# Copies out of PSUM that write runs of bf16 and read PSUM with a stride; the first chunk's weights read in place

## The chip, the cores and the metric

The kernel runs on one core of a Trainium2 chip. The metric is device time in microseconds (us) of one execution. The core's engines each take their instructions in order: TensorE (PE in the profile, its weight loads PEld), VectorE (DVE), ScalarE (ACT), GpSimd (POOL) and SyncE (SP), which here only issues DMAs. [...]

## The reference

Two independent parts share one program, and their outputs stand side by side.

```python
def _A_ref(x, wqkv, wo):                       # S=2048, D=640, H=32 heads of 20
    W, dil = 8, 2                              # 8 positions back, every second one
    qkv = (x @ wqkv) ...; q, k, v = qkv[0], qkv[1], qkv[2]
    logits = einsum("bhsd,bhswd->bhsw", q, kg) * scale    # kg, vg: gathered windows
    attn = softmax(logits); o = einsum("bhsw,bhswd->bhsd", attn, vg)
    return o.reshape(B, S, D) @ wo
def _B_ref(u, A_re, ..., log_dt, Dskip):       # L=2048, D=640, N=192
    P = exp(logdA[:, :, None] * l);  K = einsum("dn,dnl,dn->dl", Cc, P, dB).real
    Yf = rfft(pad(u)) * rfft(pad(K));  y = irfft(Yf)[:L]
    return y + u * Dskip
return concatenate([a, b], axis=-1)
```

Part A is a sliding-window attention with a dilation of 2; part B is a long convolution whose filter K is made from complex powers, carried out as a Fourier transform in two matmul steps each way.

## The kernel before

Part A projects q, k and v in `PartA.proj` (300 matmuls at L463 in groups of five, each group emptied by one of 60 ACT copies at L464), writes them to DRAM, and then works through eight blocks of 256 positions: `fetch` (DMAs, among them 20 of `vb` for each block), `logits` (DVE products at L503, matmuls at L505, softmax on ACT), `av` (DVE products at L529, matmuls at L532, ACT copies `oT` at L535) and `out_proj` (matmuls at L544, ACT copies `ob` at L545).

Part B works in five chunks of 128 channels. `Tables` holds for one chunk the tables of powers X and Y, which DVE builds by complex products (`cmul`, L260 to L265; `ypos`, `yneg`, `xtab`). `kgen` turns them into the filter with 512 small matmuls for a chunk (L342, L347) and four ACT copies into `Kd` (L349). `spread` sorts `Kd` into `K` (L372, copies at L375). `f1` and `f2` are the two steps of the forward transform: `f1` has 16 matmuls and eight ACT copies into `A1` (L385, L386); `f2` has 128 matmuls (L400) and 16 ACT copies into the spectrum `Sp` (L404). `Sp` is laid out as [half, signal, t, k] with 32 values of k next to each other; each copy of `f2` brings four k for 64 t of one signal, or for 64 t of both signals. `product` multiplies the spectra on DVE (L414, L415), `swap_halves` makes `UT` by a DMA, and `ia` is the first inverse step, with 64 matmuls (L427) and eight ACT copies into `Z` (L428), which is laid out with 32 t next to each other. `inverse` is the last step, at the end of the program, fed by DMAs of `HB`, `zq` and `uq`.

One iteration for chunk c does `swap_halves`, `spread(c)`, `f1`, `f2`, `product`, `ia`, then makes the tables and the filter of chunk c+2, then attention blocks 2c and 2c+1. The order on each engine is not that of the code: the body is scheduled by a timeline of estimated costs, so instructions of independent parts are mixed, and a changed dependence can move many of them. What is fixed by buffers: `f2`, `f1`, `ia`, `kgen` and `spread` share four PSUM buffers (tag "b"), and the tables X and Y have one buffer each, so a chunk's tables can be loaded only after the `kgen` of the chunk before.

Before the loop, the weights product `Gt` is made by DVE in `weights()`, and ACT copies its first chunk into slot 6 of `Xg` (L662), from where `xtab` reads it; the other chunks go through DRAM (`Gdram`).

A row "ACT CAST Sp<-ps_f 128x512" names line, engine and shape as the profile flattens them.

Of the kernel before, what the change touches and what calls it, by code (L numbers as in the profile page):

```python
# [250 lines left out]
def cmul(nc, O, Y, g, t, conj, rep=None):  # L251

    V = nc.vector
    sh = list(Y.shape)
    gr, gi = (g[:, r] for r in range(2))
    for _ in range(2):
        gr, gi = gr.unsqueeze(1), gi.unsqueeze(1)
    full = lambda ap: ap.rearrange("p a n r m -> p a (n r) m") if rep else ap
    gb = lambda ap: ap.to_broadcast([sh[0], sh[1], sh[2] * 2 if rep else 2, sh[-1]])
    V.tensor_tensor(out=full(O), in0=full(Y), in1=gb(gr), op=A.mult)  # L260
    V.tensor_tensor(out=full(t), in0=full(Y), in1=gb(gi), op=A.mult)
    P = [O[:, :, r] if not rep else O[:, :, :, r] for r in range(2)]
    T = [t[:, :, r] if not rep else t[:, :, :, r] for r in range(2)]
    V.tensor_tensor(out=P[0], in0=P[0], in1=T[1], op=(A.add if conj else A.subtract))
    V.tensor_tensor(out=P[1], in0=P[1], in1=T[0], op=(A.subtract if conj else A.add))  # L265


class Tables:
# [37 lines left out]
            neg = Y[:, 8 - 8 * i:16 - 8 * i, 1]  # L306
            V.tensor_scalar(out=neg, in0=neg, scalar1=-1.0, scalar2=None, op0=A.mult)

    def xtab(self):
        nc, X, Xg, tmp = self.nc, self.X, self.Xg, self.tmp()  # L310
        cmul(nc, X[:, 0:1], Xg[:, 6:7], self.Y[:, 32], tmp[:, 0:1], True)

        def xs(o, i, g):
            n = len(range(20)[i])
            cmul(nc, X[:, o], X[:, i], Xg[:, g], tmp[:, 0:n], True)

        S_ = slice
        xs(S_(1, 2), S_(0, 1), 2)
        xs(S_(2, 4), S_(0, 2), 1)
        xs(S_(4, 8), S_(0, 4), 0)  # L320
        xs(S_(8, 12), S_(0, 4), 3)
        cmul(nc, X[:, 12:16].rearrange("p (a b) r m -> p a b r m", a=2), X[:, 0:16].rearrange("p (a b) r m -> p a b r m", a=2)[:, :, 0:2], Xg[:, 4],
             tmp[:, 0:4].rearrange("p (a b) r m -> p a b r m", a=2), True, rep=2)
        xs(S_(16, 18), S_(0, 9, 8), 5)
        xs(S_(18, 20), S_(12, 15, 2), 5)

    def kgen(self):

        nc, X, Y = self.nc, self.X, self.Y
        MM = nc.tensor.matmul  # L330
        Kd = self.pools["keep"].tile([128, 2, NB, 16], bf16, name="Kd", tag="Kd", bufs=2)
        for q in range(4):
            t0 = 8 * q
            ps = self.pools["psum"].tile([128, 8, NB], f32, name="ps_k", tag="b", bufs=4)
            MM(ps[:], lhsT=self.pools["zero"], rhs=Y[:, 0:8, 0, 0:NB], start=True, stop=False, skip_group_check=True)
            for part in range(4):
                for i in range(8):
                    for g in range(4):
                        o = ps[32 * g:32 * g + 20, i, :]
                        if part < 2:  # L340
                            col = 32 * g + t0 + i
                            MM(o, lhsT=X[:, :, part, col], rhs=Y[:, :, part, col], start=False, stop=False,  # L342
                               tile_position=(0, 32 * g), skip_group_check=True)
                        else:
                            col = 128 + 32 * (g % 2) + t0 + i
                            hb = 64 * (g // 2)
                            MM(o, lhsT=X[hb:hb + 64, :, part - 2, col], rhs=Y[hb:hb + 64, :, part - 2, col], start=False, stop=(part == 3),  # L347
                               tile_position=(hb, 32 * g), skip_group_check=True)
            nc.scalar.copy(out=Kd[:, q // 2, :, 8 * (q % 2):8 * (q % 2) + 8].rearrange("p b t -> p t b"), in_=ps[:])  # L349
        for g in range(4):  # L350
            r = 32 * g
            nc.gpsimd.dma_start(out=Kd[r + 20:r + 32, :, 0:NB - 1, :].rearrange("p h b t -> p h (b t)"), in_=Kd[r + 8:r + 20, :, 1:NB, :].rearrange("p h b t -> p h (b t)"))
        return Kd
# [35 lines left out]
def f2(tc, pools, C, A1, Sp, s0, s1):  # L389

    nc = tc.nc
    n = 64 * (s1 - s0)
    for q in range(8):
        ps = [pools["psum"].tile([128, 4, n], f32, name="ps_f2", tag="b", bufs=4) for _ in range(2)]
        for kk in range(4):
            k = 4 * q + kk
            for r in range(2):
                for h in range(2):
                    hs = slice(64 * h, 64 * h + 64)
                    nc.tensor.matmul(ps[h][:, kk], lhsT=C["T"][hs, k, 64 * (1 - r):64 * (1 - r) + 128], rhs=A1[hs, k, r, s0:s1, :].rearrange("p s t -> p (s t)"),  # L400
                                     start=(kk == 0 and r == 0), stop=(r == 1), tile_position=(64 * h, 0), skip_group_check=True)
        for h in range(2):
            o = Sp[:, h, s0:s1, :, 4 * q:4 * q + 4].rearrange("p s t k -> p k (s t)")
            nc.scalar.copy(out=o, in_=ps[h][:])  # L404


def swap_halves(nc, Sp, UT):
# [10 lines left out]
def ia(tc, pools, C, P, Q, Z):  # L418

    nc = tc.nc  # L420
    for h in range(2):
        for tq in range(4):
            ps = pools["psum"].tile([128, 4, 128], f32, name="ps_ia", tag="b", bufs=4)
            for i in range(4):
                for n_, X in enumerate((P, Q)):
                    t = 4 * tq + i
                    nc.tensor.matmul(ps[:, i], lhsT=X[:, h, 4 * t:4 * t + 4, :].rearrange("p g k -> p (g k)"), rhs=C["E"][:, n_, :], start=(i == 0 and n_ == 0), stop=(n_ == 1), skip_group_check=True)  # L427
            nc.scalar.copy(out=Z[:, :, 16 * h + 4 * tq:16 * h + 4 * tq + 4].rearrange("p x t -> p t x"), in_=ps[:])  # L428


class PartA:
# [119 lines left out]
def kernel(  # L551
# [17 lines left out]
    nc = tc.nc  # L569
# [70 lines left out]
    t0 = tabs[0] = Tables(tc, pools, 0)  # L640
# [18 lines left out]
    t1.ymag(ta, pin)  # L659
    magnitudes(tc, pools, ta, am, 1, 5)  # L660
    Gt = weights()
    nc.scalar.copy(out=t0.Xg[:, 6], in_=Gt[:, 0])  # L662
    t0.xtab()
    Kds[0] = t0.kgen()
    for ct in range(5):
        a.proj("k", ct)
# [23 lines left out]
    def spec():  # L690
        return fp.tile([128, 2, 2, 64, 32], bf16, name="Sp", tag="Sp", bufs=2)

    U = uload(0)
    f1(tc, pools, C, U, "BU", A1, 1)
    SU = spec()
    f2(tc, pools, C, A1, SU, 1, 2)
    a.open(att)
    a.fetch(0)
# [26 lines left out]
    for c in range(NCH):  # L725
# [9 lines left out]
        f1(tc, pools, C, K, "BK", A1, 0)  # L735
        Sp = spec()
        f2(tc, pools, C, A1, Sp, 0, 1 if last else 2)
        product(nc, Sp, SU, UT)
        if c < 3:
            Z = fp.tile([128, 128, 32], bf16, name="Z", tag="Z")  # L740
        else:
            Z = Z34[:, c - 3]
        ia(tc, pools, C, Sp[:, :, 0], UT[:], Z)
        if c < 3:
            nc.sync.dma_start(out=Zd[c][:], in_=Z[:])
# [56 lines left out]
```

## Time and profile before

| | |
|---|---|
| time of the runs | median 681.76 us of 2 (679.98 to 683.54) |
| the profiled execution | 680.84 us, of which the span of its instructions is 679.0 us |
| mean granted clock of PE | 0.672 of full speed |
| DMA | 74.41 MB, mean 110 GB/s |
| POOL busy | 36.3 us (5%) |

A page of the profile gives each engine's busy time, the groups of equal instructions with their count, busy time in all, mean time of one and the idle time before them with what ended it, and the chain of work that ended last. "Busy" of a group counts overlapping instructions once, so the mean of one is longer than busy time divided by count where an engine starts the next before the last has ended. The program has three stretches: from 0 to about 182 us the loads, the tables of chunk 0 and 1 and the projections; to about 616 us the loop; the rest is the last step of the inverse.

### The profile page before, as it was taken

The numbers are of one execution on the slowest core, as the hardware profiler recorded it, in microseconds if no ns is written. First come the engines' busy times: TensorE is split into PE (matmuls) and PEld (weight loads), VectorE is DVE, ScalarE is ACT, GpSimd is POOL, SyncE is SP. The second block draws the span as 40 slices with busy tenths as digits, with TensorE's granted clock in tenths as the row PEclk, the third lists the DMA queues.
The fourth block names the chain that finished last, engine by engine and source line by source line (L and its number), as shares of the span: only waits on it lengthen the run. The fifth ranks groups of instructions, "written<-read, shape, count | busy, mean of one in ns | idle before, by whom it ended". The sixth has DMA issues, their size and how long they took to land.

```text
span 679.0 us, 12860 instructions
## 1 busy us (share of the span) xinstructions
PE 387.0 (57%) x5356; PEld 235.1 (35%) x5364; DVE 310.2 (46%) x479; ACT 491.4 (72%) x601; POOL 36.3 (5%) x80
## 2 busy tenths in 40 slices
PE   2764986885675536474525855437876247464422
PEld 1231453334443314343303633325533224242311
DVE  0965967691376525228635066471361412500000
ACT  3679776542699997659989569969699799793211
POOL 6500003000100000010000100000100000000000
PEclk9995988895558557567556685556676568567567
DMA  9811457547666631636201672113691050007995
GB/s 239 162 45 71 155 178 225 169 159 126 120 99 152 73 74 40 188 66 72 57 11 28 172 126 47 32 47 85 198 230 42 0 116 30 1 1 168 262 206 112
DMA packets 184761, 74.41 MB, mean 110 GB/s; under 512 B 135072, under 2 KB 176656, under 8 KB 183168
## 3 DMA queue, kind: packets, MB, share of 16 engines
q1 hardware_dynamic: 181296, 68.17, 43.6%
q0 software_dynamic: 2352, 5.18, 2.8%
q8 instruction: 42, 0.69, 0.4%
q10 hardware_dynamic: 1056, 0.25, 0.2%
q14 instruction: 15, 0.12, 0.1%
HBM read 44.20 MB, written 21.01 MB: 96 GB/s over the span
## 4 chain that ended last, share of the span: by engine, by line
ACT 46%; PE 17%; SPq 11%; DMA 10%; DVE 10%; issue 5%; DVEq 0%; POOL 0%; ACTq 0%; POOLq 0%
ACT Sp L404 25%; ACT Z L428 11%; PE ps_p L463 3%; SPq L723 3%; PE ps_op L544 3%; SPq L445 3%; SPq L685 3%; DMA Gdram<-cs 2%; PE ps_k L347 2%; ACT mag L299 2%; PE ps_k L342 2%; ACT A L386 2%; DMA uq<-in_B_u_dram 1%; DVE p L529 1%; DMA Ytab<-Gdram 1%
## 5 line engine op out<-in xcount | busy, mean ns | idle before, releaser
L404 ACT CAST Sp<-ps_f 128x512 bf16<-128x512 f32 (+1 forms) x96 | 183.8, 2331 | 4.1 <-PE ps_f L400 4.1
L400 PE MATMUL ps_f<-A,cT 64*128 64x128 bf16 (+1 forms) x768 | 62.4, 263 | 73.5 <-ACT Sp L404 70.1
L428 ACT CAST Z<-ps_ia 128x512 bf16<-128x512 f32 x40 | 92.0, 2743 | 8.9 <-PE ps_ia L427 8.8
L463 PE MATMUL ps_p<-xT,w 128*128 128x512 bf16 x292 | 79.3, 418 | 21.0 <-ACT st L464 15.1
L529 DVE TENSOR_TENSOR p<-vb,attn 128x2048 bf16<-128x2048 bf16 x40 | 47.8, 1221 | 70.9 <-PE ps_o L532 48.6
L503 DVE TENSOR_TENSOR prod<-qb,kb 128x2048 bf16<-128x2048 bf16 x40 | 47.9, 1225 | 70.1 <-PE ps_l L505 64.3
L400 PEld LDWEIGHTS <-cT 64*128 64x128 bf16 x768 | 46.1, 120 | 97.2 <-issue 97.1
L349 ACT CAST Kd<-ps_k 128x264 bf16<-128x264 f32 x20 | 25.8, 1325 | 40.7 <-PE ps_k L347 40.7
L464 ACT CAST st<-ps_p 128x512 bf16<-128x512 f32 x60 | 34.1, 582 | 27.2 <-PE ps_p L463 27.1
L463 PEld LDWEIGHTS <-w 128*128 128x128 bf16 x300 | 30.5, 105 | 64.7 <-issue 36.1
L544 PE MATMUL ps_op<-wo,oT 128*128 128x320 bf16 x160 | 43.1, 423 | 16.2 <-ACT oT L535 15.8
L427 PE MATMUL ps_ia<-cE,Sp 128*128 128x128 bf16 x160 | 30.1, 274 | 32.5 <-ACT Z L428 21.3
L721 ACT CAST ysb<-ps_ib 128x384 bf16<-128x384 f32 (+1 forms) x24 | 11.9, 523 | 46.9 <-PE ps_ib L720 33.0
L386 ACT CAST A<-ps_f 128x512 bf16<-128x512 f32 x80 | 42.0, 648 | 3.9 <-PE ps_f L385 3.8
L713 DVE TENSOR_TENSOR uq<-uq,Dsb 128x1536 bf16<-128x1536 bf16 (+1 forms) x8 | 6.6, 825 | 74.8 <-DMA uq<-in_B_u_dram 73.5
L347 PE MATMUL ps_k<-Ytab,Xtab 64*20 64x33 bf16 x1280 | 27.9, 244 | 14.9 <-issue 14.8
L414 DVE TENSOR_TENSOR UT<-Sp,UT 128x2048 bf16<-128x2048 bf16 x10 | 12.1, 1223 | 48.1 <-ACT Sp L404 48.1
L342 PE MATMUL ps_k<-Ytab,Xtab 128*20 128x33 bf16 x1280 | 27.0, 250 | 10.4 <-issue 5.8
L532 PE MATMUL ps_o<-p,cHs 128*32 128x256 bf16 x320 | 25.9, 377 | 9.6 <-DVE p L529 9.6
L427 PE MATMUL ps_ia<-cE,UT 128*128 128x128 bf16 x160 | 30.3, 275 | 0.0
L544 PEld LDWEIGHTS <-oT 128*128 128x128 bf16 x160 | 17.9, 127 | 33.3 <-ACT oT L535 18.2
L347 PEld LDWEIGHTS <-Xtab 64*20 64x20 bf16 x1280 | 22.5, 123 | 19.0 <-issue 16.8
(106 smaller groups left out, 645.6 us busy)
## 6 DMA issues: line engine op xcount, KB each, us to landing
vb<-vd SPq DMA_DIRECT2D x160, 64.5 KB, 2.2
HB<-k_HB SPq DMA_DIRECT2D x8, 1024.0 KB, 6.2
UT<-Sp SPq DMA_DIRECT2D x10, 512.0 KB, 5.6
Gdram<-cs SPq DMA_DIRECT2D x11, 288.0 KB, 2.9
Zdram<-Z SPq DMA_DIRECT2D x3, 1024.0 KB, 5.2
zq<-Zdram SPq DMA_DIRECT2D x12, 256.0 KB, 7.0
kb<-kd SPq DMA_DIRECT2D x8, 337.5 KB, 5.4
Xg<-Gdram SPq DMA_DIRECT2D x4, 672.0 KB, 6.5
```

The costliest lines, as they stand in the source:

```text
L342: MM(o, lhsT=X[:, :, part, col], rhs=Y[:, :, part, col], start=False, stop=False, tile_position=(0, 32 * g), skip_group_check=True)
L347: MM(o, lhsT=X[hb:hb + 64, :, part - 2, col], rhs=Y[hb:hb + 64, :, part - 2, col], start=False, stop=(part == 3), tile_position=(hb, 32 * ...
L386: nc.scalar.copy(out=A1[:].rearrange("p k r s t -> p (k r) s t")[:, :, sig, 8 * q:8 * q + 8], in_=ps[:])
L400: nc.tensor.matmul(ps[h][:, kk], lhsT=C["T"][hs, k, 64 * (1 - r):64 * (1 - r) + 128], rhs=A1[hs, k, r, s0:s1, :].rearrange("p s t -> p (s ...
L404: nc.scalar.copy(out=o, in_=ps[h][:])
L427: nc.tensor.matmul(ps[:, i], lhsT=X[:, h, 4 * t:4 * t + 4, :].rearrange("p g k -> p (g k)"), rhs=C["E"][:, n_, :], start=(i == 0 and n_ == ...
L428: nc.scalar.copy(out=Z[:, :, 16 * h + 4 * tq:16 * h + 4 * tq + 4].rearrange("p x t -> p t x"), in_=ps[:])
L463: nc.tensor.matmul(ps[:], lhsT=self.w[which][:, kt, 128 * ct:128 * ct + 128], rhs=self.xT[:, kt, 512 * sc:512 * sc + 512], start=(kt == 0) ...
L464: nc.scalar.copy(out=st[:, sc], in_=ps[:])
L503: V.tensor_tensor(out=pr[:], in0=q[:, ct].unsqueeze(1).to_broadcast([128, W, PB]), in1=windows(k[:, ct, 0:PB], 2, W), op=A.mult)
L529: V.tensor_tensor(out=p2[:], in0=windows(v[t][:, :, 0:PB], 2, 2), in1=at[:].unsqueeze(2).to_broadcast([128, 2, 4, PB]), op=A.mult)
L544: nc.tensor.matmul(ps[:], lhsT=oT[:, t, 128 * s:128 * s + 128], rhs=self.wo_sb[:, t, 320 * eh:320 * eh + 320], start=(t == 0), stop=(t == 4))
```

## The change

In three copies out of PSUM the two sides are exchanged: before, PSUM was read in the order in which it lies and SBUF was written with a stride; now SBUF is written in runs and PSUM is read with a stride. The destination and the values are the same, and so is the number of elements. `Kd` (L349) is now written in runs of 8 bf16, `Sp` (L404) and `Z` (L428) in runs of 4. The strides of the reads are 33 f32 in `kgen`, 64 or 128 f32 in `f2`, and 128 f32 in `ia`.

The fourth edit takes away the copy of `Gt` into `Xg`: `xtab` gets `Gt[:, 0:1]` as an argument and reads it where DVE made it.

```diff
-    def xtab(self):
+    def xtab(self, w=None):
         nc, X, Xg, tmp = self.nc, self.X, self.Xg, self.tmp()
-        cmul(nc, X[:, 0:1], Xg[:, 6:7], self.Y[:, 32], tmp[:, 0:1], True)
+        cmul(nc, X[:, 0:1], Xg[:, 6:7] if w is None else w, self.Y[:, 32], tmp[:, 0:1], True)
...
-            nc.scalar.copy(out=Kd[:, q // 2, :, 8 * (q % 2):8 * (q % 2) + 8].rearrange("p b t -> p t b"), in_=ps[:])
+            nc.scalar.copy(out=Kd[:, q // 2, :, 8 * (q % 2):8 * (q % 2) + 8], in_=ps[:].rearrange("p t b -> p b t"))
...
-            o = Sp[:, h, s0:s1, :, 4 * q:4 * q + 4].rearrange("p s t k -> p k (s t)")
-            nc.scalar.copy(out=o, in_=ps[h][:])
+            o = Sp[:, h, s0:s1, :, 4 * q:4 * q + 4].rearrange("p s t k -> p (s t) k")
+            nc.scalar.copy(out=o, in_=ps[h][:].rearrange("p k x -> p x k"))
...
-            nc.scalar.copy(out=Z[:, :, 16 * h + 4 * tq:16 * h + 4 * tq + 4].rearrange("p x t -> p t x"), in_=ps[:])
+            nc.scalar.copy(out=Z[:, :, 16 * h + 4 * tq:16 * h + 4 * tq + 4], in_=ps[:].rearrange("p t x -> p x t"))
...
-    nc.scalar.copy(out=t0.Xg[:, 6], in_=Gt[:, 0])
-    t0.xtab()
+    t0.xtab(Gt[:, 0:1])
```

The scheduled order moves with it. On DVE, after the last product of `weights()`, stood three groups of the gates `cs` of the next batch, and then the first product of `xtab`, which read `Xg`:

```order
L242 TENSOR_SCALAR ph<-wi 128x192
L247 TENSOR_TENSOR cs<-cs,am 128x384
L245 SCALAR_TENSOR_TENSOR ab<-ph 128x192
L242 TENSOR_SCALAR ph<-wi 128x192
L247 TENSOR_TENSOR cs<-cs,am 128x384
L245 SCALAR_TENSOR_TENSOR ab<-ph 128x192
L260 TENSOR_TENSOR Xtab<-Xg,Ytab 128x384
L261 TENSOR_TENSOR krtmp<-Xg,Ytab 128x384
```

Now the products of `xtab` follow at once, reading `Gt`:

```order
L260 TENSOR_TENSOR Xtab<-Gt,Ytab 128x384
L261 TENSOR_TENSOR krtmp<-Gt,Ytab 128x384
L264 TENSOR_TENSOR Xtab<-Xtab,krtmp 128x192
L265 TENSOR_TENSOR Xtab<-Xtab,krtmp 128x192
L260 TENSOR_TENSOR Xtab<-Xtab,Xg 128x384
```

So `xtab` of chunk 0 moves ahead of six gate instructions, and on PE the `kgen` of chunk 0 stands 50 projection matmuls earlier.

On ACT, at the end of the loop, the last `ia` (Z) and the first copies of `inverse` (`ysb`) had copies of the last attention block (`oT`, `ob`) between them:

```order
L404 CAST Sp<-ps_f_7320 128x4x64
L535 CAST oT<-ps_o 128x512 x2
L428 CAST Z_6126<-ps_ia 128x4x128 x4
L535 CAST oT<-ps_o 128x256
L428 CAST Z_6126<-ps_ia 128x4x128 x4
L545 CAST ob<-ps_op 128x320 x2
L721 CAST ysb<-ps_ib 128x384 x3
L545 CAST ob<-ps_op 128x320 x2
L721 CAST ysb<-ps_ib 128x384 x13
```

Now the attention copies all stand before the last `f2`:

```order
L404 CAST Sp<-ps_f_7319 128x64x4
L428 CAST Z_6125<-ps_ia 128x128x4 x8
L720 CAST ysb<-ps_ib 128x384 x16
L720 CAST ysb<-ps_ib 128x512 x8
```

What moved are five copies of the last attention block, with the matmuls that feed them. In between, the copies of attention and of the transforms are mixed in another order too, with the same members. The line numbers after L662 are lower by one in the changed kernel.

## The prediction

> **What bounds the kernel now.** I read the page's busy times first, then its chain of work that ended last, then the same chain and the busy times for the loop alone.
>
> ```profile
> span 679.0 us, 12860 instructions
> PE 387.0 (57%) x5356; PEld 235.1 (35%) x5364; DVE 310.2 (46%) x479; ACT 491.4 (72%) x601; POOL 36.3 (5%) x80
> ...
> ACT 46%; PE 17%; SPq 11%; DMA 10%; DVE 10%; issue 5%; DVEq 0%; POOL 0%; ACTq 0%; POOLq 0%
> ```
>
> ACT is the busiest engine and holds 46% of the chain. The busy times by stretch (columns: stretch, its length, PE, PEld, DVE, ACT and POOL with counts, granted clock, DMA share, GB/s) show where:
>
> ```profile
> 0.00:182.00 182.00, 120.48 (x1526) 61.67 (x1536) 113.62 (x230) 108.28 (x221) 28.90 (x64) 0.83 0.57 151
> 182.00:616.00 434.00, 248.41 (x3593) 159.41 (x3588) 191.87 (x243) 372.21 (x358) 7.38 (x16) 0.60 0.37 80
> 616.00:679.00 63.00, 18.13 (x247) 13.97 (x245) 4.68 (x6) 10.92 (x22) 0.00 (x0) 0.69 0.86 196
> 218.00:255.00 37.00, 15.35 (x141) 9.39 (x141) 17.05 (x24) 37.00 (x20) 0.00 (x0) 0.50 0.50 74
> ```
>
> In the loop (182 to 616) ACT is busy for 372 of 434 us; in one `f2` (218 to 255) it is busy without a gap, while PE idles at a clock of 0.50. The start and the end are bound by other things: in the last 63 us the DMA engines are at 0.86 and ACT at 11 us. The chain of the loop alone, and its longest pieces (start, length, what):
>
> ```profile
> by line: ACT Sp L404 38.8%; ACT Z L428 17.8%; issue 6.3%; PE ps_op L544 4.0%; PE ps_k L347 3.8%; PE ps_k L342 3.4%; ACT A L386 2.6%; DVE p L529 1.9%; ACT mag L299 1.8%; DMA Ytab<-Gdram 1.4%; DMA out_dram<-ob 1.3%; PE ps_ia L427 1.3%; DVE kr
> ...
> 422.61 22.43 ACT Sp L404 x10
> 541.76 18.10 ACT Z L428 x8
> ```
>
> So 38.8% and 17.8% of 434 us, 168.4 + 77.3 = 245.7 us, are two of the changed copies, back to back, with nothing else ending last. The other 188.3 us of the loop are everything else.
>
> **The price of a copy.** The groups of ACT's copies out of PSUM, with mean times:
>
> ```profile
> L404 ACT CAST Sp<-ps_f 128x512 bf16<-128x512 f32 x64 | 146.3, 2724 | 1.8 <-PE ps_f L400 1.8
> L428 ACT CAST Z<-ps_ia 128x512 bf16<-128x512 f32 x40 | 92.0, 2743 | 8.9 <-PE ps_ia L427 8.8
> L386 ACT CAST A<-ps_f 128x512 bf16<-128x512 f32 x80 | 42.0, 648 | 3.9 <-PE ps_f L385 3.8
> L404 ACT CAST Sp<-ps_f 128x256 bf16<-128x256 f32 x32 | 37.5, 1546 | 2.4 <-PE ps_f L400 2.4
> L464 ACT CAST st<-ps_p 128x512 bf16<-128x512 f32 x60 | 34.1, 582 | 27.2 <-PE ps_p L463 27.1
> L349 ACT CAST Kd<-ps_k 128x264 bf16<-128x264 f32 x20 | 25.8, 1325 | 40.7 <-PE ps_k L347 40.7
> ```
>
> All read PSUM in order. L464 writes without a gap, L386 in runs of 8 bf16, and both are near 0.6 us for 512 elements. L404, L428 and L349 write every element apart from the next, and cost over four times as much. What is slow is the lone write. Back to back, a copy of 512 takes 146.3/64 = 2.29 us and one of 256 takes 37.5/32 = 1.17 us, so a lone element costs (2.29 − 1.17)/256 = 4.4 ns, and a copy in runs of 8 goes at 42.0/80 = 0.525 us, 1.03 ns per element.
>
> Runs of 4 appear nowhere. From below: they can't beat runs of 8, 0.525 us. From above: a run could cost what its elements did singly, 2.29 us. I take one lone-write price per run, 128 × 4.4 ns = 0.56 us: that is close to the row of L386, where 64 such prices would be 0.28 us and the stream of elements sets the time. For 256 elements it is about 0.30 us, for `Kd` (runs of 8) 0.525 × 264/512 = 0.27 us.
>
> The read is the unknown. No row here reads PSUM with a stride. From below it costs nothing (L464's rate), from above I know only the lone write of 4.4 ns; it could be more, since nothing excludes it. I take nothing, because the nearest rows, L464 and L386, read the same f32 from PSUM at about 1 ns per element, and what made L404 slow was on the side of the write.
>
> [...]
>
> **The sum.** When ACT no longer ends last in these stages, PE does. Its pace is in these rows: with free buffers, and waiting for ACT in pieces of eight (L427 likewise from the chain):
>
> ```profile
> 409.71 1.89 PE L400 MATMUL ps_f<-A,cT 64*128 64x128 bf16 x32
> ...
> 415.51 1.01 PE L400 MATMUL ps_f<-A,cT 64*128 64x128 bf16 x8 [1.24 <-ACT Sp L404]
> ...
> 181.49 1.03 PE L400 MATMUL ps_f<-A,cT 64*128 64x64 bf16 x32
> 453.09 1.05 PE ps_ia L427 x8
> ```
>
> 1. `f2` on both signals, four times: 16 copies × 0.56 = 9.0 us on ACT; 128 matmuls on PE at 1.89/32 = 0.059 us take 7.6 us, at up to 0.107 us 13.7. I take 14, with the hand-overs between the four PSUM buffers: 56 us.
> 2. `f2` on one signal, twice: 16 × 0.30 = 4.8 us against 128 × 1.03/32 = 4.1 us. I take 7: 14 us.
> 3. `ia`, five times: 8 × 0.56 = 4.5 us against 64 matmuls, eight in about 0.8 before their tail, so 6.4 us. I take 7: 35 us.
>
> These 105 us stand where 245.7 stood: 140.7 us go.
>
> 4. Given back: work that lay under the copies. The waits of the loop and one chunk's stretch:
>
> ```profile
> DVE prod L503 <- PE ps_l L505: 64.3, 12, 13.9
> DVE UT L414 <- ACT Sp L404: 48.1, 7, 14.7
> ...
> 313.00:410.00 97.00, 49.99 (x860) 32.07 (x861) 49.40 (x70) 79.02 (x82) 2.61 (x6) 0.60 0.41 76
> 389.10 6.19 DMA Ytab<-Gdram
> ```
>
> A period of 97 us holds 49.4 us of DVE and 50.0 of PE. Taking out (37 − 14) + (18 − 7) leaves about 63 us. Both still fit, but DVE is then 78% busy, and its chain has a fixed part: tables come by DMA only after the `kgen` before (6.19 us), DVE builds them between attention products, and only then the next `kgen` runs. What is late next is DVE's products and PE behind them. I give back 5 us for each of four periods, 20 us; ends 0 (all fits) and 50 us (no overlap regained: half of the 88 us of DVE that lie inside the four `f2` windows).
>
> 5. `Kd`: 20 copies lose about 1 us each, but 16 of them wait for PE (the group's idle time, 40.7 us, is longer than its 25.8 us of work); on the chain 1 us appears in the first stretch. I take 0.
> 6. The copy of `Gt` and `xtab`:
>
> ```profile
> 54.23 1.16 DVE L211 TENSOR_TENSOR Gt<-pr,pr 128x960 bf16<-128x960 f32 x1
> 62.72 0.26 DVE L242 TENSOR_SCALAR ph<-wi 128x192 int32<-128x192 int32 x1 [7.33 <-ACT cs L244]
> ...
> 63.54 0.49 ACT L662 COPY Xg<-Gt 128x384 bf16<-128x384 bf16 x1
> ...
> 90.79 1.28 PE L342 MATMUL ps_k<-Ytab,Xtab 128*20 128x33 bf16 x64
> ```
>
> `Gt` is ready at 55.4, the copy runs at 63.5, and DVE idles for 7.33 us between. `xtab` will start some 9 us earlier in that gap, and the first `kgen` (90.79) can follow 50 matmuls earlier. But the stretch ends with all projections done on PE, whose total doesn't change, and with the loads behind them. I take 0, ends −5 and +3.
> 7. The tail: the five attention copies that leave the last `ia` were free there; the loads that bound the last 63 us stay. 0.
>
> The profiled execution took 680.84 us, of which 1.84 lie outside the span; it is 0.9 below the median of two runs. 680.84 − 140.7 + 20 = 560.1. I forecast 560 us.
>
> **The rivals.**
>
> [...]
>
> *Nothing gained.* If a strided read costs as much as a lone write, 4.4 ns, the copy stays at 2.29 us and the time at 681 us. For it: one such penalty is in these rows already, on the other memory. Against it: that is the extreme of what a row shows.
>
> *Slower.* If a strided read costs more than the lone write, ACT still ends last, and the 245.7 us grow in proportion. At 5 ns per element they grow by 14%, to 280 us: 715 us. It decides from 4.65 ns on, where the growth of 5.6% on 245.7 us is 2% of the whole.
>
> *All of it.* If copies go at 0.525 us, PE at 0.059 us and nothing is given back, `f2` takes 9.5 and 5, `ia` 5: 73 us, a gain of 173, 508 us. Against it: PE and DVE both need more than half of the shrunken period.
>
> **How the numbers follow.** The forecast's case (copies near 0.56 us, 530 to 585 us) has a chance of 0.62; the first rival (585 to 630) 0.18; all of it (below 530) 0.06; nothing gained 0.07; slower 0.07. A range from 520 to 615 leaves out the last two, the upper edge of the first rival and the lower of the fourth, about 0.2. About 2% is what a measurement of this kernel can tell from no change: faster 0.62 + 0.18 + 0.06 = 0.86, within 2% 0.07, slower 0.07.
>
> **What would show it.** Right: the groups of L404 and L428 have means below 0.85 us and busy times near 0.6 us per copy; the chain of the loop has PE and DVE ahead of ACT; the granted clock in the `f2` windows is above 0.50, since PE no longer waits in pieces; `Xtab` starts right behind `Gt` near 55 us; the last stretch stays near 63 us. Wrong: means of L404 at 1 us or more say that the strided read has a price; copies that are cheap but a loop above 340 us say that item 4 is too small, and the waits of DVE and SP would name what came in; a start longer than 185 us says that the moved `kgen` isn't free.

## The result, and the profile after

The changed kernel takes 535.55 us (median of 2 runs, 535.35 to 535.75) against 681.76 us: a ratio of 0.7855, 95% interval 0.7766 to 0.7945. The forecast was 560 us with a range of 520 to 615.

The page's busy times and its chain of work that ended last, after the change:

```profile
span 533.6 us, 12869 instructions
PE 339.5 (64%) x5364; PEld 216.2 (41%) x5364; DVE 308.6 (58%) x479; ACT 268.9 (50%) x600; POOL 36.2 (7%) x80
...
PE 24%; DVE 23%; SPq 20%; DMA 13%; ACT 9%; issue 9%; DVEq 0%; POOL 0%; ACTq 0%; POOLq 0%
```

ACT lost 222.5 us of busy time and fell from 46% of the chain to 9%. PE has the same instructions and yet 47.5 us less busy time, which the sum had not counted. Busy times by stretch, as before the change cut where the first `f2` begins and where `inverse` begins:

```profile
0.00:185.00 185.00, 120.70 (x1514) 60.96 (x1514) 114.50 (x230) 101.27 (x220) 28.82 (x64) 0.82 0.58 151
185.00:470.00 285.00, 198.31 (x3615) 139.42 (x3609) 189.37 (x243) 156.75 (x359) 7.38 (x16) 0.75 0.57 119
470.00:533.60 63.60, 20.52 (x244) 15.82 (x242) 4.69 (x6) 10.92 (x21) 0.00 (x0) 0.58 0.85 194
```

The whole gain lies in the loop, 434 to 285 us. The start is 3 us longer, the end 0.6. In the loop PE is busy 198 us at a granted clock of 0.75, where it was 248 us at 0.60. The loop's chain is now spread over many small pieces, none above 11.3%:

```profile
by line: issue 11.3%; DVE p L529 10.1%; PE ps_ia L427 6.0%; PE ps_k L347 5.5%; PE ps_k L342 5.3%; DVE krtmp L261 5.1%; DVE prod L503 4.5%; SPq L493 3.7%; PE ps_op L544 3.2%; PE ps_f L400 3.0%; DVE Xtab L260 2.9%; DMA Ytab<-Gdram 2.9%; DVE U
```

The copies themselves, and one `f2` of both signals, one of a single signal and the last `ia` in order of time:

```profile
L386 ACT CAST A<-ps_f 128x512 bf16<-128x512 f32 x80 | 42.1, 627 | 12.6 <-DMA vb<-vd 7.6 <-PE ps_f L385 4.7
L404 ACT CAST Sp<-ps_f 128x512 bf16<-128x512 f32 x64 | 33.5, 615 | 7.6 <-PE ps_f L400 7.6
L428 ACT CAST Z<-ps_ia 128x512 bf16<-128x512 f32 x40 | 22.1, 592 | 28.5 <-PE ps_ia L427 28.1
L404 ACT CAST Sp<-ps_f 128x256 bf16<-128x256 f32 x32 | 9.5, 408 | 5.8 <-PE ps_f L400 5.7
L349 ACT CAST Kd<-ps_k 128x264 bf16<-128x264 f32 x20 | 7.6, 378 | 61.1 <-PE ps_k L347 61.1
...
420.19 2.05 ACT L404 CAST Sp<-ps_f 128x512 bf16<-128x512 f32 x4 [1.95 <-PE ps_f L400]
...
430.03 1.13 ACT L404 CAST Sp<-ps_f 128x512 bf16<-128x512 f32 x2
454.26 4.52 ACT L404 CAST Sp<-ps_f 128x256 bf16<-128x256 f32 x16 [0.48 <-PE ps_f L400]
463.25 0.59 ACT L428 CAST Z<-ps_ia 128x512 bf16<-128x512 f32 x1 [4.46 <-PE ps_ia L427]
...
466.66 2.05 ACT L428 CAST Z<-ps_ia 128x512 bf16<-128x512 f32 x4 [0.27 <-PE ps_ia L427]
```

Back to back a copy of 512 into `Sp` now takes 33.5/64 = 0.523 us, as much as one into `A1` in runs of 8 (42.1/80 = 0.526); before, it was 2.29. In this `ia` each of the first four copies into `Z` (0.59 us) is followed by a wait of 0.27 us for PE and the last four run back to back, so PE sets the pace for most of it; in the `f2` of one signal ACT still runs its 16 copies without a gap.

### The profile page after: what moved, and what is told of

Its sections match the earlier page's. It is cut to its first block, busy times and chain, and to the rows that moved or that the text cites. A ratio compares the mean times of both kernels' runs of the same rounds, so it can differ in the third digit from the quotient of the medians.

```text
span 533.6 us, 12869 instructions
## 1 busy us (share of the span) xinstructions
PE 339.5 (64%) x5364; PEld 216.2 (41%) x5364; DVE 308.6 (58%) x479; ACT 268.9 (50%) x600; POOL 36.2 (7%) x80
## 4 chain that ended last, share of the span: by engine, by line
PE 24%; DVE 23%; SPq 20%; DMA 13%; ACT 9%; issue 9%; DVEq 0%; POOL 0%; ACTq 0%; POOLq 0%
DVE p L529 5%; PE ps_p L463 5%; PE ps_k L347 4%; SPq L493 4%; SPq L684 4%; PE ps_k L342 4%; SPq L445 3%; PE ps_ia L427 3%; DMA uq<-in_B_u_dram 3%; SPq L710 3%; SPq L722 3%; DVE krtmp L261 3%; DVE prod L503 3%; DMA Ytab<-Gdram 2%; DVE Ytab L305 2%
## 5 line engine op out<-in xcount | busy, mean ns | idle before, releaser
L463 PE MATMUL ps_p<-xT,w 128*128 128x512 bf16 x300 | 80.6, 422 | 20.1 <-ACT st L464 13.9
L404 ACT CAST Sp<-ps_f 128x512 bf16<-128x512 f32 (+1 forms) x96 | 43.0, 546 | 13.4 <-PE ps_f L400 13.3
L386 ACT CAST A<-ps_f 128x512 bf16<-128x512 f32 x80 | 42.1, 627 | 12.6 <-DMA vb<-vd 7.6
L532 PE MATMUL ps_o<-p,cHs 128*32 128x256 bf16 x320 | 23.4, 346 | 33.8 <-DVE p L529 33.7
L400 PE MATMUL ps_f<-A,cT 64*128 64x128 bf16 (+1 forms) x768 | 37.4, 237 | 5.9 <-ACT A L386 5.4
L400 PEld LDWEIGHTS <-cT 64*128 64x128 bf16 x768 | 32.2, 110 | 16.2 <-issue 15.3
L349 ACT CAST Kd<-ps_k 128x264 bf16<-128x264 f32 x20 | 7.6, 378 | 61.1 <-PE ps_k L347 61.1
L260 DVE TENSOR_TENSOR Ytab<-Ytab 128x384 bf16<-128x384 bf16 (+2 forms) x15 | 13.3, 889 | 42.0 <-DMA Ytab<-Gdram 27.7
L428 ACT CAST Z<-ps_ia 128x512 bf16<-128x512 f32 x40 | 22.1, 592 | 28.5 <-PE ps_ia L427 28.1
L716 PE MATMUL ps_ib<-uq,cident 128*128 128x384 bf16 (+1 forms) x24 | 11.4, 477 | 37.6 <-DVE uq L712 37.6
L544 PE MATMUL ps_op<-wo,oT 128*128 128x320 bf16 x160 | 32.2, 337 | 4.3 <-ACT oT L535 2.5
L347 PEld LDWEIGHTS <-Xtab 64*20 64x20 bf16 x1280 | 22.1, 123 | 19.6 <-issue 17.4
L342 PEld LDWEIGHTS <-Xtab 128*20 128x20 bf16 x1280 | 22.6, 128 | 14.3 <-issue 12.0
```

What stands on the lines that cost most here:

```text
L386: nc.scalar.copy(out=A1[:].rearrange("p k r s t -> p (k r) s t")[:, :, sig, 8 * q:8 * q + 8], in_=ps[:])
L404: nc.scalar.copy(out=o, in_=ps[h][:].rearrange("p k x -> p x k"))
L463: nc.tensor.matmul(ps[:], lhsT=self.w[which][:, kt, 128 * ct:128 * ct + 128], rhs=self.xT[:, kt, 512 * sc:512 * sc + 512], start=(kt == 0) ...
L532: nc.tensor.matmul(ps[32 * q:32 * q + 32, t % 2], lhsT=C["Hs"][:], rhs=p2[:, m, q, :], start=(t % 2 == 0 and m == 0), stop=(m == 1), tile_ ...
L544: nc.tensor.matmul(ps[:], lhsT=oT[:, t, 128 * s:128 * s + 128], rhs=self.wo_sb[:, t, 320 * eh:320 * eh + 320], start=(t == 0), stop=(t == 4))
```

## The experiments

The order on PE, ACT, DVE and SP turned out to depend on the `Gt` edit alone: with it, the scheduled order is that of the changed kernel, without it that of before, whatever the copies do. So the two halves of the change can be had apart, each in its own order: the traces of experiments 2 to 4 have the order of before on these engines, those of 1 and 5 to 7 the order of the changed kernel. In experiments 8 to 11 the order moves on all four engines as well, so each of them shows its edit together with an order that it brings.

**1. The weights alone.** Before, with only the fourth edit:

```diff
-    def xtab(self):
+    def xtab(self, w=None):
...
-        cmul(nc, X[:, 0:1], Xg[:, 6:7], self.Y[:, 32], tmp[:, 0:1], True)
+        cmul(nc, X[:, 0:1], Xg[:, 6:7] if w is None else w, self.Y[:, 32], tmp[:, 0:1], True)
...
-    nc.scalar.copy(out=t0.Xg[:, 6], in_=Gt[:, 0])
-    t0.xtab()
+    t0.xtab(Gt[:, 0:1])
```

> Before, with only the weights of chunk 0 read from Gt; the copies are the old ones, the order on every engine is that of the changed kernel. Theory (the gain is the price of the copies): within 1% of before, 675 to 688 us, the copies of Sp still near 2.7 us. Rival (the new order brings a good part of the gain): 660 us or less.

Measured: 697.29 us, ratio to before 1.0245 (1.0202 to 1.0288). Both theories miss: the new order brings no gain, and it is not neutral either. Stretches cut at the same two places:

```profile
0.00:187.50 187.50, 121.94 (x1506) 61.24 (x1514) 114.49 (x230) 107.83 (x220) 28.98 (x64) 0.83 0.57 149
187.50:633.00 445.50, 252.78 (x3601) 162.76 (x3598) 191.03 (x243) 371.91 (x357) 7.40 (x16) 0.61 0.36 76
```

The start is 5.5 us longer, the loop 11.5, at the same busy time of ACT. The attention copies that now stand ahead of the last `f2` and `ia` are not where the time goes. From the first matmul of the last `f2` to the last copy of the last `ia` this kernel takes 40.0 us, 4.2 less than before (44.2). It had fallen behind by then: its third `f2` begins 3 us earlier than before (307.9 against 311.1), its fifth 23 us later (521.3 against 498.5). Just ahead of that fifth `f2` its chain shows loads, which do not end last there in the kernel before:

```profile
507.83 7.92 DMA uq<-in_B_u_dram
515.82 8.21 DMA vb<-vd
```

So the loss arises in the middle of the loop. Which of the moved instructions make it was not tried.

**2. The copies alone.** Before, with only the three exchanged copies.

> Before, with only the three copies changed; the order on every engine is that of before. Theory (copies): 525 to 545 us, within 2% of the changed kernel; a few us below it if the earlier kgen of chunk 0 costs the 4 us by which the first f2 came later. Rival (order): 560 us or more.

Measured: 533.99 us, ratio to before 0.7853 (0.7806 to 0.7899).

```profile
0.00:182.00 182.00, 121.96 (x1506) 61.81 (x1514) 113.44 (x230) 101.73 (x221) 28.78 (x64) 0.83 0.56 150
182.00:468.00 286.00, 199.91 (x3609) 137.32 (x3602) 190.22 (x243) 155.40 (x357) 7.40 (x16) 0.74 0.57 121
```

The copies carry the whole gain. The start is 182 us, as before, and the loop is the same as in the changed kernel to 1 us. The 3 us lost at the start come with the `Gt` edit: the first `f2` begins at 181.5 to 184.9 us in the four profiled kernels with the order of before, at 185.2 to 188.3 in the five with the order of the changed kernel. With fast copies the two orders can't be told apart by the time: both ratios are 0.785.

**3. Sp alone.**

```diff
-            o = Sp[:, h, s0:s1, :, 4 * q:4 * q + 4].rearrange("p s t k -> p k (s t)")
-            nc.scalar.copy(out=o, in_=ps[h][:])
+            o = Sp[:, h, s0:s1, :, 4 * q:4 * q + 4].rearrange("p s t k -> p (s t) k")
+            nc.scalar.copy(out=o, in_=ps[h][:].rearrange("p k x -> p x k"))
```

> Before, with only the copy into Sp (L404) changed. Theory (each copy's place on the chain is worth its own term): 168 us of chain become about 60, so 570 to 590 us, and Z still at 2.7 us each. Rival (the work that was under these copies comes out and takes half of it back): 600 us or more.

Measured: 579.30 us, ratio 0.8504 (0.8451 to 0.8557), in the theory's range. `Sp` is worth 100.5 of the 146 us. The six stages `f2`, each from its first matmul to its last copy, shrink from 196 us in all to 75, and the loop from 434 to 329 us, so some 17 us came back as work that had lain under the copies; the rival had expected about half. `Z` and `Kd` together bring the other 45.

**4. Sp and Z, without Kd.** As 2, with the copy into `Kd` as before.

> Before, with the copies into Sp and Z changed, and those into Kd as before. Theory (the copies into Kd wait for PE and are worth nothing): 530 to 540 us, as with all three changed. Rival (now that ACT no longer covers it, kgen stands on the chain and its copies with it): 545 us or more.

Measured: 535.34 us, ratio 0.7853 (0.7823 to 0.7884). The `Kd` copies are slow and cost nothing that these runs can tell (535.34 against 533.99 us in experiment 2, with overlapping intervals):

```profile
L349 ACT CAST Kd<-ps_k 128x264 bf16<-128x264 f32 x20 | 25.5, 1276 | 68.4 <-PE ps_k L347 68.4
```

ACT waits 68.4 us for PE ahead of 25.5 us of work, as the prediction argued.

**5. The price of the strided read.** In the changed kernel the copy of the projections gets a strided read and keeps its gapless write:

```diff
-            nc.scalar.copy(out=st[:, sc], in_=ps[:])
+            nc.scalar.copy(out=st[:, sc].rearrange("p (x k) -> p x k", k=4), in_=ps[:].rearrange("p (k x) -> p x k", k=4))
```

> The changed kernel, with the copies of the projections (L464) reading PSUM with a stride of 128 f32 and writing SBUF without a gap; q, k and v come out with their positions permuted, so part A is not the reference's. Theory (the strided read is free): mean of L464 570 to 600 ns, time as the changed kernel. [...]

Measured: 534.65 us (one run). The group, in this kernel and in the changed one:

```profile
L464 ACT CAST st<-ps_p 128x512 bf16<-128x512 f32 x60 | 34.3, 581 | 26.3 <-PE ps_p L463 26.3
```

```profile
L464 ACT CAST st<-ps_p 128x512 bf16<-128x512 f32 x60 | 34.4, 582 | 28.2 <-PE ps_p L463 28.2
```

581 against 582 ns: reading f32 from PSUM with a stride of 128 costs ACT nothing here.

**6. Runs of two.** The changed kernel, `Sp` and `Z` in runs of 2 bf16:

```diff
-            o = Sp[:, h, s0:s1, :, 4 * q:4 * q + 4].rearrange("p s t k -> p (s t) k")
-            nc.scalar.copy(out=o, in_=ps[h][:].rearrange("p k x -> p x k"))
+            o = Sp[:, h, s0:s1, :, 4 * q:4 * q + 4].rearrange("p s t (a b) -> p a (s t) b", b=2)
+            nc.scalar.copy(out=o, in_=ps[h][:].rearrange("p (a b) x -> p a x b", b=2))
... (and likewise in ia)
```

> The changed kernel, with Sp and Z written in runs of 2 bf16 instead of 4; PSUM is read with a stride all the same. Theory (one lone-write price of 4.4 ns for each run, hidden only where the run's own elements take longer): 256 runs x 4.4 = 1.13 us per copy of 512 back to back, and about 560 to 575 us. Rival (two neighbours are enough to hide it): 0.52 us as with runs of 4, and no change of the time.

Measured: 538.76 us (one run); the theory falls.

```profile
L404 ACT CAST Sp<-ps_f 128x512 bf16<-128x512 f32 x64 | 34.1, 630 | 7.3 <-PE ps_f L400 7.3
L428 ACT CAST Z<-ps_ia 128x512 bf16<-128x512 f32 x40 | 22.7, 608 | 26.7 <-PE ps_ia L427 26.6
```

34.1/64 = 0.533 us: two neighbours are about as good as four (0.523 us) or eight (0.526 us). One price for each run is not how it works: it would have given 1.13 us.

**7. Pairs that aren't neighbours.** Do the two bf16 have to be neighbours, or is it enough that they lie near each other? Two at a time again, but 4 bytes apart (`"p s t (a b) -> p b (s t) a"` in the place of the pattern above, and likewise in `ia`).

> The changed kernel, with Sp and Z written two bf16 at a time that lie 4 bytes apart, so that no two written one after the other are neighbours, but both lie within 8 bytes. [...]

Measured: 576.65 us (one run).

```profile
L404 ACT CAST Sp<-ps_f 128x512 bf16<-128x512 f32 x64 | 75.0, 1373 | 5.8 <-PE ps_f L400 5.8
L404 ACT CAST Sp<-ps_f 128x256 bf16<-128x256 f32 x32 | 18.8, 809 | 4.2 <-PE ps_f L400 4.2
```

75.0/64 = 1.17 us and 18.8/32 = 0.59: more than twice the 0.533 us of pairs of neighbours and about half of the 2.29 us of lone elements. The difference gives (1.17 − 0.59)/256 = 2.3 ns per element, 4.6 ns per pair, while a lone element cost 4.4 ns and a pair of neighbours costs 2 × 1.04 = 2.1. So a pair that lies 4 bytes apart pays about the lone price once, and a pair of neighbours doesn't pay it. The neighbours of experiment 6 also start at a multiple of 4 bytes in their tile each time, so these runs can't tell whether that counts or the adjacency alone; a pair of neighbours that starts 2 bytes off was not tried, and no distance but this one.

**8 and 9. What bounds the loop now.** Two kernels leave out work, one on DVE and one on SP's queue. First 32 of 40 products of the logits:

```diff
         for ct in range(5):
-            pr = p.tile([128, W, PB], bf16, name="prod", tag="prod", bufs=2)
-            V.tensor_tensor(out=pr[:], ...)
+            if ct == 0:
+                pr = p.tile([128, W, PB], bf16, name="prod", tag="prod", bufs=2)
+                V.tensor_tensor(out=pr[:], ...)
```

> The changed kernel, with the DVE product of the logits made only for the first of five channel tiles and used for all five: 32 of 40 products of 1.22 us are left out (39 us of DVE), so part A is not the reference's. Theory (DVE bounds the loop now): 15 to 39 us less. Rival (the SP queue and the loads bound it): less than 8 us.

Measured: 520.34 us (one run), 15.2 below the changed kernel, the lower edge of the theory. DVE's busy time fell by 36.5 us (308.6 to 272.1), of which 21 brought nothing. A longer wait of DVE for the tables would account for them, 27.7 us in the changed kernel and here:

```profile
DVE Ytab L260 <- DMA Ytab<-Gdram: 52.9, 4, 31.4
```

Then four of five loads of v (`for t in range(1)`, one tile used five times):

> The changed kernel, with v fetched for one of five channel tiles and used for all five: 128 of 160 loads of vb are left out (some 60 us of SP's queue at 0.47 us each), so part A is not the reference's. Theory (DVE bounds the loop now): under 15 us less, most of it at the first block, where DVE waits 26 us for vb. Rival (SP's queue): 25 us less or more.

Measured: 532.81 us (one run), 2.7 below the changed kernel, which one run can't tell from nothing. The wait of the first block, from which the theory expected most of a gain, is still there, with a fifth of the loads (26.2 us in the changed kernel):

```profile
DVE p L529 <- DMA vb<-vd: 26.9, 1, 26.9
```

So the number of loads of v is not the bound; the loads of `U` stayed on SP's queue, so the queue itself is not ruled out (experiment 11). Of the two, less work on DVE brings more, but not the whole of what is left out, and either run has an order of its own.

**10. vb issued by ACT.** `nc.sync.dma_start` becomes `nc.scalar.dma_start` for the 160 loads of `vb`.

> The changed kernel, with the 160 loads of vb issued by ACT's queue instead of SP's. Theory (at the first block vb stands behind the loads of U on SP's queue): 5 to 15 us less, since vb no longer waits for U. Rival (the DMA engines, not the queue, are what the loads wait for): within 4 us of the changed kernel; or slower by as much as ACT spends on issuing.

Measured: 555.19 us, ratio to before 0.8164 (0.8131 to 0.8197), 19.6 us worse than the changed kernel. The rival's second half holds: ACT pays for the issuing, and besides it waits for `vb` without issuing (64.8 − 40.2 = 24.6 us, below). The largest of ACT's new waits, and one of its seven in order of time:

```profile
ACT oT L535 <- DMA vb<-vd: 38.8, 7, 7.3
...
233.14 6.56 ACTq L493 DMA_DIRECT2D vb<-vd  x13
239.74 0.58 ACT L535 CAST oT<-ps_o 128x512 bf16<-128x512 f32 x1 [6.04 <-DMA vb<-vd]
```

Thirteen issues in a row take 6.56 us, and ACT is idle for 6.04 us until the last of them is out, although the matmuls whose result it copies next had ended at 235.1. All of ACT's idle stretches that end with `vb` add up to 64.8 us; in 40.2 of these ACT's queue was issuing, and the rest is waiting. How much of the 19.6 us is the new order was not tried.

**11. U issued by POOL.** The copies alone (2), and the 40 loads of `U` by `nc.gpsimd.dma_start`.

> The three copies changed, the weights as before, and the 40 loads of U issued by POOL's queue instead of SP's. Theory (at the start of the loop vb and the tables of the next chunk wait on SP's queue behind U): 4 to 12 us less than with the three copies alone (533.99). Rival (the DMA engines, busy with rows of 32 bytes, are what they wait for): within 4 us, or slower.

Measured: 526.71 us, ratio to before 0.7665 (0.7590 to 0.7739); the interval lies below that of 2. By the medians the gain over 2 is 7 us, by the two ratios 13. Its four runs spread from 519.19 to 530.91, more than those of any other kernel here. POOL issues eight loads in 8.4 us, where SP's eight took 19.5 us in the changed kernel:

```profile
147.90 8.36 POOL L685 DMA_DIRECT2D U<-in_B_u_dram  x8
```

```profile
154.16 19.54 SPq L684 DMA_DIRECT2D U<-in_B_u_dram  x8
173.81 11.33 SPq L493 DMA_DIRECT2D vb<-vd  x20
```

But the first `f2` of this kernel comes at 192.9 us, later than the 182.3 of 2; the gain is made in the loop after it, so the theory's place is wrong even where its size fits, and the new order may be part of it. This is the fastest kernel that computes everything.

## Why the prediction was right, and where it was off

**What was slow.** Shown: the lone bf16 write, not the amount of data (512 elements back to back in 2.29 us before, in 0.523 us in runs of 4 and 0.533 us in runs of 2; experiments 2, 5, 6). The groups came out as forecast for the right case, with `Sp` and `Z` below 0.85 us.

**Price of a copy.** 0.56 us was forecast for 512 elements and 0.523 (`Sp`) and 0.553 (`Z`) came; 0.30 against 0.297 for 256; for `Kd` 0.27 against 0.38. The value was near, the reasoning behind it wrong: "one lone-write price per run" would have given 1.13 us in experiment 6, where 0.533 was measured. It gave nearly the right number for runs of 4 because 4.4 ns is close to the time that four elements take anyway (4 × 1.03 = 4.1 ns by the row of L386). That is luck.

**The strided read.** Taken as nothing, and shown to be nothing (experiment 5: 581 against 582 ns). That removes the rivals "nothing gained" and "slower". The chance of 0.18 for 585 to 630 us stood on a strided read with a price of its own, and no run shows one: the copies into `Sp` and `Z` took 0.523 and 0.553 us.

**Items 1 to 3 of the sum.** 105 us were forecast for the transforms' stages. Each stage measured from its first matmul to the end of its last copy:

| stage | before, us | after, us | forecast for after |
|---|---|---|---|
| `f2`, both signals | 38.6, 41.4, 37.6, 39.1 | 11.4, 14.7, 10.2, 12.0 | 14 each |
| `f2`, one signal | 19.6, 20.1 | 11.1, 5.0 | 7 each |
| `ia` | 18.8, 19.2, 20.6, 19.2, 19.4 | 7.2, 7.0, 6.0, 7.1, 6.5 | 7 each |
| in all | 293.5 | 98.2 | 105 |

So the stages came out near the forecast. The mean granted clock in the four `f2` of both signals rose from between 0.50 and 0.60 to between 0.67 and 0.88, as the signs had it.

**What they replace, and item 4.** Here the sum compares two different things. The 105 us are whole stages, but the 245.7 us that they replace are only what the copies had on the chain; the same stages lasted 293.5 us before, with 47.8 us of other steps in them. Stage against stage, the gain is 195.3 us and not 140.7. Item 4 errs the other way: the rest of the loop grew from 434 − 293.5 = 140.5 us to 285 − 98.2 = 186.8, so 46.3 us came back and not 20, close to the upper end that the forecast gave it. (The 88 us of DVE behind that end are those of four wider stretches, 177 us in all; in the `f2` themselves DVE is busy for 67.) The two misses, 54.6 and 26.3 us, work against each other, and that the time came out within 25 us of the forecast owes something to this. The work under the copies did move into view, as item 4 said: between 201 and 232 us DVE is busy for 29.40 of 31 us.

```profile
201.00:232.00 31.00, 19.77 (x230) 12.67 (x231) 29.40 (x41) 23.20 (x56) 0.00 (x0) 0.78 0.72 132
```

**PE and its clock.** The sum left out that PE itself becomes faster, although the clock stands among the signs to look for. In the loop PE is busy for 50 us less. Half of this is in `f2` itself (62.4 to 37.4 us at L400), whose matmuls no longer come in pieces of eight. But matmuls that no edit touches are faster as well, such as those of attention's output, before and after:

```profile
L544 PE MATMUL ps_op<-wo,oT 128*128 128x320 bf16 x160 | 43.1, 423 | 16.2 <-ACT oT L535 15.8
```

```profile
L544 PE MATMUL ps_op<-wo,oT 128*128 128x320 bf16 x160 | 32.2, 337 | 4.3 <-ACT oT L535 2.5 <-ACT ob L545 1.7
```

The traces tell why. The granted clock changes between 0.50 and 1.00 and nothing between, and the same matmul has the same two times in both kernels: before, from 217 to 260 us (clock 0.50) and from 391 to 400 us (clock 1.00), then after, from 156 to 193 us (0.50) and from 221 to 234 us (1.00):

```profile
L544 PE MATMUL ps_op<-wo,oT 128*128 128x320 bf16 x18 | 5.5, 467 | 6.3 <-ACT oT L535 6.1 <-ACT ob L545 0.2
L544 PE MATMUL ps_op<-wo,oT 128*128 128x320 bf16 x15 | 2.5, 300 | 0.0
...
L544 PE MATMUL ps_op<-wo,oT 128*128 128x320 bf16 x8 | 2.5, 468 | 0.0
L544 PE MATMUL ps_op<-wo,oT 128*128 128x320 bf16 x20 | 3.4, 300 | 0.6 <-ACT ob L545 0.4 <-ACT oT L535 0.2
```

The mean fell because 124 of the 160 now run wholly at the full clock, where it was 42. That the clock rose because PE waits less for ACT fits all this but is argued, and what it was worth in time is open: no run holds the clock still.

**Items 5 to 7.** `Kd` at nothing: shown, as far as experiment 4 can tell. The `Gt` edit at nothing, −5 to +3 us: 3 us later in the start of the changed kernel, at the edge; in the time of the changed kernel it doesn't show. By itself it costs 17.5 us beside slow copies (experiment 1), which item 6 would not have found: it looked at the start alone, and most of that loss is in the loop. The tail at nothing: 63.6 against 63 us; the copies that left it are seven by the listed order, not five.

**The account.** 679.0 − 533.6 = 145.4 us of span: 195.3 us from the stages, less 46.3 given back in the rest of the loop, 3 at the start and 0.6 at the end. The forecast was 140.7 less 20, that is 120.7.

## What to carry to other kernels

When a copy out of PSUM transposes, let the strided side be the read of PSUM and let at least two bf16 stand next to each other in SBUF (0.533 us for 512 elements here, where lone ones took 2.29). A row that is four times as slow as another of the same shape is read by what differs in its pattern, and the two ends of the pattern are priced apart by a copy that has only one of them. In such a sum, put whole stages against whole stages, or shares of the chain against shares of the chain, not one against the other. When a bound engine is relieved, look whether PE's clock has changed too (0.60 to 0.75 in the loop here), and try each half of a change in the order that it brings, since an edit of one small copy moved hundreds of instructions here.

## What the runs showed of the hardware

- ACT wrote a bf16 that stands alone, 64 bytes from the next, in 4.4 ns (before: 2.29 us for 512, 1.17 for 256), a pair of neighbours in 2.1 (experiment 6), and a pair 4 bytes apart in 4.6 (experiment 7). A copy of 512 took 0.533 us in pairs of neighbours, about as long as in runs of 4 (0.523) and of 8 (0.526); in pairs 4 bytes apart it took 1.17.
- ACT read f32 from PSUM with a stride of 128 as fast as in order (581 and 582 ns for a copy of 512, experiment 5).
- The granted clock of PE was either 0.50 or 1.00 in the traces of before and after, and a matmul of 128x320 took 467 and 300 ns with it, before and after alike.
- Loads issued by ACT took time from ACT's own work: 13 loads of `vb` in a row took 6.56 us, in 6.04 of which ACT was idle (experiment 10). Moving 160 of them to ACT's queue cost 19.6 us, together with the order that came with it.
